# Small vector steps given a choice of engine, and the first batch's x kept as fp16 pairs, in a two-stage attention kernel

## The chip, the cores and the metric

The kernel runs on one core of one Trainium2 chip. The metric is the device time of one execution in microseconds (us); of several timed executions the median counts. Lower is better.

## The reference

Two stages follow each other. In the first, each of 8 batches and 8 heads has 512 tokens `x` and 32 state rows `state` of 64 elements; the tokens attend to the state rows and the state rows to the tokens. Their results, 544 rows for each batch, are the input of the second stage: a causal attention with four experts, each with its own q, k, v and output matrix, of which a gate picks two for each row.

```
scores  = x @ state.T / 8;   xread = softmax(scores) @ state
scores2 = state @ x.T / 8;   sread = softmax(scores2) @ x
x = concat([xread, sread])            # 8 x 544 x 512
logits = x @ w_gate                   # 4 experts, the best 2 are kept: weights w
for e in range(4):
    q, k, v = x @ wq[e], x @ wk[e], x @ wv[e]
    a  = softmax(causal(q @ k.T / 8))
    out += (e is picked) * w * (a @ v @ wo[e])
```

The q and k weights are large, so that the scores of the second stage spread widely and small errors in them would show. The kernel therefore carries nearly every operand of a matmul as a pair of fp16 numbers, a high part and the remainder, and multiplies pairs in three passes (high by high, high by low, low by high). "hi_lo" in the code makes such a pair: ScalarE rounds to the high part, VectorE (or GpSimd) subtracts it from the source to get the low part.

## The kernel before

**Names.** TensorE is PE in the profile, VectorE is DVE, ScalarE is ACT, GpSimd is POOL, and SP issues the DMAs. All instructions but a few constants are recorded first and issued by one loop in `Steps.run`, so nearly every instruction has line L265; tiles tell them apart.

**How the work is cut.** One batch is the unit. `front(b)` does the first stage for the 512 tokens of a batch (four blocks of 128, index `t`; two halves, index `u`) and forms the inputs of the second: `xn` is x as loaded (two buffers, one for each half of the tokens), `xh` its fp16 pair, `xT` the transposed pair, `bd` the transposed state pair; `eb` holds the scores and then the softmax of tokens over state rows, with `mb` the maxima and `sbm` the sums; `at` is that softmax transposed. Because the softmax has only 32 columns for each head, the products with wq, wk, wv and w_gate are first applied to the state (`gs`, "bank<-wn,bd" or, in the first batch, "bank<-p,bd" from the weights as loaded), and then `at` times `gs` gives v, k, q and the gate's logits `lg` ("bank<-gs,at", "bank<-at,gs"). `gate` turns logits into expert weights `wgt`, with `gs` also the name of its small sums. `m6` ("m<-wgt") masks q, `qf`/`qh`/`qm` are q, its pair and its transpose, `kt_` is k.

`side(b)` is the attention of state rows over tokens: `state_scores` gives `e2` ("e"), with `m2` ("m<-m") the scaled maxima and `s2` ("s") the sums, then `a2`, its transpose `a2t`, and the product with `xh`, kept in `xt_tail`.

`probs(b, unit)` does the second stage's scores for one block of tokens (or two): `mx` are the negated maxima of each row, `shifted` adds a constant to them, ACT takes exp with `mx` as bias and sums into `su`, `p` are the probabilities, `ph` their pair, and a DMA transpose gives `pt`. `su` is then inverted and multiplied with the expert weights to `c6` ("c<-su,wgt"). `reads` multiplies `pt` with v, weighs the result by `c6` (tile `z`), transposes it by DMA (`z<-zh`) and applies wo. `tail` does the same for the 64 state rows of two batches at a time; its tiles begin with t (`tmx`, `tqf`, `ptl`).

**First batch.** `whole = b < CFG["FB"]` is true for batch 0 alone. There x, the softmax and `gs` are kept whole in fp32 and multiplied in one fp32 pass, not in three fp16 passes; x is transposed on PE, straight from `xn` (lines 511 to 517), later batches' x by DMA. Since `side(0)` needs `xh` anyway, batch 0's pairs are made late, just before it (lines 675 to 677). The logits of batch 0 have a matmul step of their own (lines 624 to 628), ahead of the v products.

**What sets the order.** Three packed tables in `ORDER` (line 22) say in which order the recorded steps are issued, which way each step runs where `st.either` gave it several (for example ACT or DVE), and which buffer slot each tile gets. Each engine, and the SP queue with its DMAs, takes its own instructions strictly in that order; a step waits for the steps that wrote its inputs or last used its slot. Before the change the small steps, such as `shifted` (line 766) and the sums' epsilon (lines 571, 705, 756, 811), had one way only, VectorE.

Of the kernel before, what the change touches and what calls it, by code (L numbers as in the profile page):

```python
# [35 lines left out]
        "EL+t_zxoQ6vTfBgw%wpFmZV7L``Wi5_KV_CD@Y)n~_s<T8ay?1ua9N-W0+|uqAb%<;dKTwqQ6C?o2DN7e(V^_>+%f6kdrDFgkao09NWlF*yd"
        "u=57>~WAQFog`vC^S7SWhgH<^q=HWOTpS#m;*@khs8n3}U@{99wc-o7*buIR#d~DQ%NcJJiKR%BAC_wgVevTsh5kv&#H=jq90^FaX$_X@yK+"
        ")t67v#UZ0~4^zNxX=AGznk8?HFBZNI1EK)w!mGmqdIDBS;LXC5ibmj-{BAjBCp-jVOC1GRBgmT!WMIVX4WH@R+3FD_BQr@c|h}`=mCf;qjD^"
        "Q*tVvKyxTHr{zEnqjVfw_Dd$-#B*sPrRRAxi8AnHT0uu-GjHW7bX<<gR5~abxvos3Eqq9}@d2Dq^<+CQpqaE!GxH9fP77%_ucZ2N8nf_0+{3"
        "eI6)mEyyp-1SYTC(rIUCQWHMENt(^Wi!*?Auq;kC4ka`1j$PC<NtXHZTq#vAw`Z=_s&h&S>k%FU&?5Fh5kyqS)0Q7*$L<R};Ch;)ogb0mo`W"  # L40
        "jPWpp%NTfB2yB%h6$u3CzAb|RFX>^DaQ@u9A3v1au(N7TuCUwT%J!#VreXgHJNOoW7<ScNkiFB@njoakP6&Lw$ep8MeFIT9H2XLkZ$5RIW2d"
        "ksGN~YatKe;cDg4U=n$2VlX{$wXfZj#m*tG6lrwaakLyuQD<!44oYGT#MKVaRjI+~xUarbv%pzxa2L;Lv%qZ#PEZ5<)lu7PORynQbIGdd3)R"
        "I|t(gR5&7dVw1rgM~DPG~MUt9ALI)Z<;0UF!2yy2MB5B9FK8)PRrDWzHd2xFM&}YjTy_@FPj9*C|jR%XPU%H{_gN<3^lYdT@~3lpA!NZ&F)s"
        "%y}fIG~sr9gPU?0xy{Wuo!;c#)SmBfPj1c~IKB4bj(m*vP)p7$x2O|epsxHx4rn<!PIoz<wBpKgP<wM{zD<2NL|Sux>C4@?fOO}5bc+khA-y"
        "GqWFQxo7CeZHNGTc2rRBC{(DG76UdTPps9pG}T%?y$R$j|1c_t_64!w~}^juC*sASUne3vT7d40fDr61p?w{lG@N;G}Q_vnLM(08(zKFW2Cs"
        "r~sfMc2z(NiOPpxujQg2tU?GdR52sFs>#~G?reWnLLzZ=l~Am*!ol_aAv)svw1kr;%9nOtIH>OuGut;j^G)VUB5|Iy`^(_BL9+%Hj=-~56NU"
        "RZMNOkQ9Qx^$!`g>pE8M?%0&AklkBfd=BYNzGTU6fqc3!{&SOy2DSTJINHe*oFZHuDm#?yfNyq3bHEki|bgZ_N``SuI^JHr+OF4^8u{Of`i0"
# [12 lines left out]
        "=1p+3ROc~vj()jZ5Acy*uXHN2)*^vYhzYk6(2<NpCb5Wk)"  # L60
    ),
    (
        "c-pO%(H4Xt2t>X7|3`1Tof2KZz^n%&P-X_SH9a_<rz7Kg`cL27W=0RZke`KcTOru;8!P`mF}Dhn&%<?GNXBXOAU#Oq;!#r6z;Wh4CX&ERfqZ"
        ")L4O6^2LA~?3(zfBC;81|0vQ=px`qJz6HBkvIR15y5@?w-iRVW2ViOF^uTiv_ty@-0vqQW3n9n;>_)k=Y^s6<DO#eytZ5Tm&JS#6Vme^!vWe"
        ">~CFi{J#By*k||8=`&y%ZLER"
    ),
# [202 lines left out]
def state_read_then_moe_attention(ctx: ExitStack, tc: tile.TileContext, x, state, w_gate, wq, wk, wv, wo, out):  # L269
# [214 lines left out]
    def front(b):  # L484
# [190 lines left out]
        if whole:  # L675
            for t in range(T):
                parts_of_x(t)
# [339 lines left out]
```

## Time and profile before

| | |
|---|---|
| three timed executions | 331.65, 333.86 and 335.05 us; median 333.86 |
| the profiled execution | 330.36 us |
| its span in the trace | 328.6 us |
| outside the span | 330.36 - 328.6 = 1.8 us |
| instructions in the span | 9140 |
| busy: PE, DVE, ACT, POOL | 288.2, 270.1, 219.3, 159.5 us |

The span runs from the first to the last instruction that the profile shows. Busy time of an engine is the time in which at least one of its instructions was under way. A row of the timeline gives start and duration in us, engine, line, operation, tiles and count of merged instructions; in brackets stands how long the engine had been idle before it, and what released it. A row of grouped instructions ends with the total busy time, the mean duration in ns of one, and the idle time before them.

### The profile page before, as it was taken

What the parts mean: (1) busy time and instruction counts of PE and PEld (TensorE: products, weight loads), DVE (VectorE), ACT (ScalarE), POOL (GpSimd) and SP (SyncE); (2) the same over time, 40 slices, a digit from 0 to 9 for tenths busy, and PEclk for the clock granted to TensorE, in tenths of its full rate; (3) what the DMA queues carried; (4) which work ended last, traced back from release to release, by engine and by line L of the source; (5) the groups of instructions that cost most, each with busy time, mean ns of one, the idle gap of its engine ahead of it and who ended that gap; (6) DMA issues with size and microseconds to landing.
All of it is one profiled execution on the core that took longest, in us unless ns stands there. A gap on an engine that the chain in (4) does not pass through costs nothing.

```text
span 328.6 us, 9140 instructions
## 1 busy us (share of the span) xinstructions
PE 288.2 (88%) x3358; PEld 199.2 (61%) x3358; DVE 270.1 (82%) x819; ACT 219.3 (67%) x642; POOL 159.5 (49%) x199
## 2 busy tenths in 40 slices
PE   7959947998298998998897998997999899999882
PEld 6727726666256565865573677755775667576551
DVE  0388988989999999999999989898999968676420
ACT  2185555769467885877966869677868748647741
POOL 5043081369475578824884496365856510242100
PEclk9965985999699999999999999999999999999998
DMA  7905796998978799699999899989889958886973
GB/s 178 168 12 158 165 174 131 179 238 149 240 143 163 144 210 182 138 185 182 235 209 204 132 195 169 172 135 188 174 168 157 181 118 145 159 149 113 166 164 96
DMA packets 165540, 53.95 MB, mean 164 GB/s; under 512 B 144504, under 2 KB 160888, under 8 KB 165496
## 3 DMA queue, kind: packets, MB, share of 16 engines
q1 hardware_dynamic: 165496, 53.38, 87.5%
q8 instruction: 26, 0.43, 0.5%
q14 instruction: 18, 0.15, 0.1%
HBM read 11.02 MB, written 8.91 MB: 61 GB/s over the span
## 4 chain that ended last, share of the span: by engine, by line
DVE 24%; PE 19%; DMA 12%; ACT 10%; issue 6%; POOL 3%; POOLq 0%; SPq 0%; ACTq 0%; DVEq 0%
PE bank L265 19%; DMA a2t<-a 4%; DVE mx L265 3%; DMA pt<-ph 3%; DVE eb L265 3%; DMA xT<-xh 3%; ACT z L265 2%; DVE gs L265 2%; DVE sbm L265 2%; ACT xh L265 1%; DMA qm<-qh 1%; DMA z<-zh 1%; DVE et L265 1%; ACT p L265 1%; DVE z L265 1%
## 5 line engine op out<-in xcount | busy, mean ns | idle before, releaser
L265 PE MATMUL bank<-gs,at 128*128 128x260 f16 (+3 forms) x384 | 52.7, 288 | 1.6 <-DVE m L265 1.6
L265 PE MATMUL bank<-v,pt 128*128 128x192 f16 x480 | 44.9, 251 | 9.4 <-DMA pt<-ph 8.7
L265 PE MATMUL bank<-wo_n,z 128*128 128x512 f16 x192 | 46.0, 380 | 3.7 <-DMA z<-zh 3.7
L265 PE MATMUL bank<-kt,qm 128*128 128x128 f16 (+7 forms) x384 | 47.9, 301 | 1.1 <-DMA qm<-qh 0.9
L265 PEld LDWEIGHTS <-pt 128*128 128x128 f16 x480 | 40.3, 100 | 13.9 <-DMA pt<-ph 11.9
L265 ACT ACTIVATE p<-bank,mx 128x128 f32<-128x128 f32 (+3 forms) x64 | 33.4, 528 | 18.3 <-DVE mx L265 15.6
L265 PEld LDWEIGHTS <-at 128*128 128x128 f16 x336 | 31.7, 97 | 9.4 <-issue 3.8
L265 DVE TENSOR_REDUCE mx<-bank 128x1 f32<-128x128 f32 (+3 forms) x64 | 29.3, 478 | 5.5 <-PE bank L265 5.5
L265 POOL TENSOR_TENSOR z<-z 128x128 f32<-128x128 f32 x24 | 13.7, 572 | 39.8 <-ACT z L265 28.1
L265 POOL TENSOR_TENSOR ph<-p,ph 128x768 f16<-128x768 f32 (+1 forms) x13 | 24.1, 1855 | 16.2 <-ACT ph L265 10.2
L265 PEld LDWEIGHTS <-z 128*128 128x128 f16 x192 | 17.6, 98 | 23.3 <-DMA z<-zh 5.0
L265 PEld LDWEIGHTS <-qm 128*128 128x128 f16 (+1 forms) x384 | 23.2, 97 | 14.0 <-DMA qm<-qh 1.4
L265 ACT ACTIVATE z<-bank,c 128x64 f32<-128x64 f32 x126 | 29.4, 332 | 2.8 <-DVE z L265 2.2
L265 PE MATMUL bank<-at,gs 128*128 128x512 f16 (+1 forms) x92 | 25.3, 419 | 0.0
L265 ACT ACTIVATE o<-bank 128x512 f32<-128x512 f32 x34 | 20.5, 602 | 6.4 <-PE bank L265 6.3
L265 POOL TENSOR_TENSOR qh<-qf,qh 128x768 f16<-128x768 f32 x11 | 18.7, 1700 | 2.8 <-ACT qh L265 2.2
L265 ACT ACTIVATE ph<-p 128x768 f16<-128x768 f32 (+1 forms) x20 | 18.6, 931 | 1.3 <-DMA pt<-ph 0.9
L265 ACT ACTIVATE xh<-xn 128x512 f16<-128x512 f32 x32 | 19.3, 640 | 0.1
L265 ACT ACTIVATE gs<-bank 128x512 f16<-128x512 f32 (+3 forms) x36 | 14.4, 458 | 5.3 <-PE bank L265 5.2
L265 DVE TENSOR_TENSOR qf<-bank,m 128x384 f32<-128x384 f32 x32 | 16.5, 548 | 1.0 <-PE bank L265 0.6
L265 POOL TENSOR_TENSOR zh<-z,zh 128x256 f16<-128x256 f32 x19 | 14.0, 741 | 5.4 <-ACT zh L265 3.9
L265 POOL TENSOR_TENSOR eb<-eb,sbm 128x512 f32<-128x512 f32 x7 | 8.1, 1164 | 16.6 <-ACT bd L265 13.2
(189 smaller groups left out, 669.5 us busy)
## 6 DMA issues: line engine op xcount, KB each, us to landing
xn<-in_x_dram SPq DMA_DIRECT2D x16, 512.0 KB
out_dram<-o SPq DMA_DIRECT2D x64, 128.0 KB
sn<-in_state_dram SPq DMA_DIRECT2D x16, 32.0 KB
p<-in_moe_wo_dram SPq DMA_DIRECT2D x2, 256.0 KB
out_dram<-o SPq DMA_DIRECT2D x2, 256.0 KB
z<-zh SPq DMA_TRANSPOSE x29
xT<-xh SPq DMA_TRANSPOSE x28
p<-in_moe_wq_dram SPq DMA_DIRECT2D x1, 384.0 KB
```

Of the source, the lines that this page charges most:

```text
L265: f(**{k: v.ap() if isinstance(v, View) else v for k, v in kw.items()})
```

## The change

1. **Choice of engine.** Two helpers, `small` (a scale and an addition on a few numbers of each partition) and `pair` (a product of two small tiles), record steps that may run on DVE, ACT or POOL (`pair`: DVE or POOL). The steps on `mx`, `sbm`, `su`, `s2`, `m2`, `tmx`, the gate's sum, `c6` and the q mask `m6` use them or a like choice.
2. **First batch.** x is split into pairs at once for all batches; batch 0 transposes the pairs on PE (8 fp16 transposes for a block into one bank, two copies out of it), and its two score steps take the usual three fp16 passes. Softmax and `gs` of batch 0 stay in fp32.
3. **Logits with values.** In batch 0 the weights wv and w_gate go through one bank, as do wq and wk, and the logits come out of the v products as 4 further columns; the separate logits step is gone.
4. **Another order.** All three tables of `ORDER` are new.

```diff
+    def small(n, out, in_, add, mul=1.0):
+        st.either([("DVE", 0.065 + n * 0.00104, (nc.vector.tensor_scalar, dict(out=out, in0=in_, scalar1=add, scalar2=mul, op0=ALU.add, op1=ALU.mult))),
+                   ("ACT", 0.1 + n * 0.000833, (nc.scalar.activation, dict(out=out, in_=in_, func=AF.Copy, bias=add * mul, scale=mul))),
+                   ("POOL", 0.17 + n * 0.00084, (nc.gpsimd.tensor_scalar, dict(out=out, in0=in_, scalar1=add, scalar2=mul, op0=ALU.add, op1=ALU.mult)))])
+    def pair(n, **kw):
+        st.either([("DVE", 0.065 + n * 0.00104, (nc.vector.tensor_tensor, kw)), ("POOL", 0.24 + n * 0.001887, (nc.gpsimd.tensor_tensor, kw))])
...
         for t in range(T):
-            if whole:
+            parts_of_x(t)
+            if b < CFG["PX"]:
                 tp = bank("xt")
-                st.mm([(tp[HC[c], j * P:(j + 1) * P], xn[t // 2][:, 2 * j + c, t % 2 * D:(t % 2 + 1) * D], ident, True, True) for j in range(H // 2) for c in range(2)],
-                      (8, 4 * P, 128, 2), into=[xT[:, t]])
+                ts = tp.bitcast(F16).rearrange("p (a j q) -> p a j q", a=2, j=H // 2)
+                st.transposes([(ts[:, a, j, :], xh[t // 2][:, t % 2, a, j * P:(j + 1) * P]) for a in range(2) for j in range(H // 2)],
+                              identh, 0.43, into=[xT[:, t]])
                 marks["t"] = len(st.all) - 1
-                out_of_bank(512, xT[:, t].rearrange("p j q -> p (j q)"), tp, 128.0)
+                for a in range(2):
+                    kw = dict(out=xT[:, t, a], in_=ts[:, a])
+                    st.either([("ACT", 0.478, (nc.scalar.activation, dict(func=AF.Copy, scale=1.0, **kw))), ("DVE", 0.6, (nc.vector.tensor_copy, kw))])
...
-                if whole:
-                    st.mm([(scs[c][:, t * P + j * NS:t * P + (j + 1) * NS], xT[HC[c], t, j, :], bd32[HC[c], HJ[j]], True, True)
-                           for t in range(2 * u, 2 * u + 2) for j in range(H // 2) for c in range(2)], (16, 4 * NS, 64, 2), into=[eb])
-                    continue
...
-            dve(16, nc.vector.tensor_scalar, out=sm[:, r], in0=sm[:, r], scalar1=EPS, scalar2=2.0 ** -12, op0=ALU.add, op1=ALU.mult)
+            small(16, sm[:, r], sm[:, r], EPS, 2.0 ** -12)
...
-        if whole:
-            lp = bank("lg")
-            st.mm([m for t in range(T) for m in chain((lp[:, t * E:(t + 1) * E], at[:, g, tok[t]], gs[:, g, NW - E:NW]) for g in range(2))],
-                  (2 * T, 52, 128, 1))
-            act(T * E, lg.rearrange("p t e -> p (t e)"), lp[:, :T * E])
         for t in range(T):
             vp = bank("vp")
-            product(vp, tok[t], QK, QK + E * D if whole else NW, [v[:, :, t]])
-            if not whole:
-                act(E, lg[:, t], vp[:, E * D:E * D + E])
+            product(vp, tok[t], QK, NW, [v[:, :, t]])
+            act(E, lg[:, t], vp[:, E * D:E * D + E])
...
-            dve(12, nc.vector.tensor_scalar, out=m6[:, :, 1 - s], in0=wgt[:, :, 3 * s:3 * s + 3], scalar1=0.0, scalar2=0.5 ** 15, op0=ALU.is_gt, op1=ALU.mult)
+            st.either([("DVE", 0.078, (nc.vector.tensor_scalar, kw)), ("POOL", 0.18, (nc.gpsimd.tensor_scalar, kw))])
...
-            dve(1, nc.vector.tensor_scalar, out=m2[:, g:g + 1], in0=m2[:, g:g + 1], scalar1=2.0 ** -17, scalar2=None, op0=ALU.mult)
+            small(1, m2[:, g:g + 1], m2[:, g:g + 1], 0.0, 2.0 ** -17)
...
-        dve(2, nc.vector.tensor_scalar, out=s2, in0=s2, scalar1=EPS, scalar2=2.0 ** -14, op0=ALU.add, op1=ALU.mult)
+        small(2, s2, s2, EPS, 2.0 ** -14)
...
     def shifted(n, mx):
-        dve(n, nc.vector.tensor_scalar, out=mx, in0=mx, scalar1=LN, scalar2=None, op0=ALU.add)
+        small(n, mx, mx, LN)
...
-        dve(2 * nb, nc.vector.tensor_scalar, out=su, in0=su, scalar1=EPS * 2.0 ** 15, scalar2=None, op0=ALU.add)
+        small(2 * nb, su, su, EPS * 2.0 ** 15)
         dve(28, nc.vector.reciprocal, out=su, in_=su)
-        dve(6 * nb, nc.vector.tensor_tensor, out=c6, in0=su.unsqueeze(2).broadcast_to([P, 2 * nb, 3]),
+        pair(6 * nb, out=c6, in0=su.unsqueeze(2).broadcast_to([P, 2 * nb, 3]),
```

What the new tables do is seen in the instructions of each engine. Counted over the whole program, DVE has 821 instructions before and 722 now, ACT 556 and 582, POOL 204 and 255. Of the 144 small steps that were DVE's (`mx` 24, `m<-m` 16, `m<-wgt` 16, `sbm` 16, `su` 24, `s` 8, the gate's sum 12, `tmx` 4, `c<-su,wgt` 24), 36 stay there, 55 are on ACT and 53 on POOL. Of the larger steps, 10 more z products and 6 more `a` low parts are on DVE, and 30 z activations fewer on ACT.

The first place is the SP queue, in the first batch. `xn` rows are loads of x, `p` rows loads of weights, `sn` loads of state; `xn_88` and `xn_89` are the two buffers of x, so their second appearance loads batch 1. Before:

```order
L265 DMA sn_87<-in_state_dram 128x1x64
L265 DMA p_1_109<-in_moe_wk_dram 128x12x64
L265 DMA p_2_110<-in_moe_wv_dram 128x12x64
L265 DMA sn_87<-in_state_dram 128x1x64 x5
L265 DMA xn_88<-in_x_dram 128x8x128
L265 DMA xn_89<-in_x_dram 128x8x128
L265 DMA p_0_108<-in_moe_wo_dram 128x512
L265 DMA_TRANSPOSE xT_95<-xh_93 128x8x128
```

And now:

```order
L265 DMA p_1_111<-in_moe_wk_dram 128x12x64
L265 DMA p_0_110<-in_moe_wq_dram 128x4x64
L265 DMA xn_88<-in_x_dram 128x8x128
L265 DMA xn_89<-in_x_dram 128x8x128
L265 DMA sn_87<-in_state_dram 128x1x64 x4
L265 DMA xn_88<-in_x_dram 128x8x128
L265 DMA_TRANSPOSE xT_97<-xh_95 128x8x128 x2
L265 DMA p_0_110<-in_moe_wo_dram 128x512
```

The loads of batch 1 stand right behind the weights, and a third load of x stands ahead of the first transposes.

The second place is DVE at the start of the first batch, from its first step on data to the last subtraction of the maxima. `bd` is the state pair, `xh_93` and `xh_94` the pairs of the two halves of x. Before:

```order
L265 TENSOR_SCALAR xT_95<-bank_83 128x512
L265 TENSOR_SCALAR xT_95<-bank_84 128x512
L265 TENSOR_REDUCE mb_112<-bank_86 128x16
L265 TENSOR_REDUCE mb_112<-bank_85 128x16
L265 TENSOR_TENSOR eb_111<-bank_86,mb_112 128x512
L265 TENSOR_TENSOR eb_111<-bank_85,mb_112 128x512
```

And now:

```order
L265 SCALAR_TENSOR_TENSOR bd_90<-bank_79,bd_90 128x128
L265 SCALAR_TENSOR_TENSOR xh_93<-xn_88,xh_93 128x512 x2
L265 SCALAR_TENSOR_TENSOR xh_94<-xn_89,xh_94 128x512
L265 COPY xT_97<-bank_81 128x512
L265 SCALAR_TENSOR_TENSOR xh_94<-xn_89,xh_94 128x512
L265 COPY xT_97<-bank_83 128x512
L265 COPY xT_97<-bank_84 128x512
L265 TENSOR_REDUCE mb_114<-bank_86 128x16
L265 TENSOR_REDUCE mb_114<-bank_85 128x16
L265 TENSOR_TENSOR eb_113<-bank_85,mb_114 128x512
L265 TENSOR_TENSOR eb_113<-bank_86,mb_114 128x512
```

The four low parts of x, which stood among the later work, are now ahead of the first maxima, between the loads and the scores.

The third place is a step of `probs` in the middle of the kernel, the third block of tokens of batch 3 (its maxima are in `mx_154` before and in `mx_156` now). DVE before:

```order
L265 TENSOR_REDUCE mx_154<-bank_82 128x1
L265 TENSOR_REDUCE gt_0_123<-cmp_122 128x16
L265 TENSOR_REDUCE mx_154<-bank_85 128x1
L265 TENSOR_TENSOR ptl_197<-p_0_108,ptl_197 128x640
L265 SCALAR_TENSOR_TENSOR tsu_196<-tsu_196 128x1
L265 SCALAR_TENSOR_TENSOR a_0_146<-e_0_140,s_1_144,a_0_146 128x512
L265 TENSOR_SCALAR mx_154<-mx_154 128x2
```

The same step on ACT now:

```order
L265 ACTIVATE tmt_190<-bank_83 128x256
L265 ACTIVATE mx_156<-mx_156 128x2
L265 ACTIVATE p_2_112,su_160<-bank_86,mx_156 128x384
L265 ACTIVATE zh_175<-z_1_169 128x256
L265 ACTIVATE tq_192<-tqf_191 128x256
L265 ACTIVATE p_2_112,su_160<-bank_79,mx_156 128x384
```

The addition on `mx` has left DVE and stands on ACT directly ahead of the exponential that reads it.

More of the change, by code (lines that the diff above doesn't have):

```diff
@@ L59 @@
[L59 to L72 removed]
+        "c-jrrgJKX06adico0p9(+ja}fwr$(?(z0#awr$(Cd+&V2K_FldP%y{~1)vZ(02G995COtN9>@>*ASy(JNDvF+Lo|pCu^}o(hX9BIaUcdHfS3"
@@ L488, in front @@
         f32 = ("bitcast", (F32,), {})
[L490 removed]
+        bd = st.buf("bd", [P, 2, P], F16, bufs=2)
         tp = bank("tp")
[L492 removed]
+        st.transposes([(tp[:, :P], sn[:, b % 2].rearrange("p c d -> p (c d)"))], ident, 0.11, into=[bd])
+        hi_lo(P, bd[:, 0], bd[:, 1], tp[:, :P], 128.0)
         if whole:
[L494 removed]
+            bd32 = st.buf("bd32", [P, P], bufs=CFG["FB"])
             act(P, bd32, tp[:, :P], scale=128.0)
[L496 to L497 removed]
         xh = [st.buf("xh", [P, 2, 2, DM], F16, bufs=CFG["xh"], use=u) for u in range(2)]
[L500 to L501 removed]
+        xT = st.buf("xT", [P, T, 2, H // 2, P], F16, bufs=1)
         def parts_of_x(t):
@@ L618, in product @@
             if whole:
-                st.mm(chain((out[:, :n], at[:, g, t], gs[:, g, lo_:hi_]) for g in range(2)), (2, 4 * n, 128, 1), into=into)
+                st.mm(chain((out[:, :n], at[:, g, t], gs[:, g, lo_:hi_]) for g in range(2)), (2, 4 * n + 230, 128, 1), into=into)
             else:
@@ L646, in front @@
             if whole:
-                st.mm(chain((pp, gs[:, g, cols], at[:, g]) for g in range(2)), (2, 4 * S, 128, 1), into=[kt_[:, :, pr, :]])
+                st.mm(chain((pp, gs[:, g, cols], at[:, g]) for g in range(2)), (2, 4 * S + 230, 128, 1), into=[kt_[:, :, pr, :]])
             else:
@@ L653, in front @@
         for s in range(2):
-            dve(12, nc.vector.tensor_scalar, out=m6[:, :, 1 - s], in0=wgt[:, :, 3 * s:3 * s + 3], scalar1=0.0, scalar2=0.5 ** 15, op0=ALU.is_gt, op1=ALU.mult)
+            kw = dict(out=m6[:, :, 1 - s], in0=wgt[:, :, 3 * s:3 * s + 3], scalar1=0.0, scalar2=0.5 ** 15, op0=ALU.is_gt, op1=ALU.mult)
+            st.either([("DVE", 0.078, (nc.vector.tensor_scalar, kw)), ("POOL", 0.18, (nc.gpsimd.tensor_scalar, kw))])
         for u in range(2):
@@ L674, in front @@
                 load_wo(marks["l"])
-        if whole:
-            for t in range(T):
-                parts_of_x(t)
-        side(b, bd32 if whole else bd, xT, xh, whole)
+        side(b, bd, xT, xh)
         st.behind = None
@@ L755, in gate @@
         dve(m, v.tensor_reduce, out=s1, in_=t2, axis=AX.X, op=ALU.add)
-        dve(n, v.tensor_scalar, out=s1, in0=s1, scalar1=EPS, scalar2=0.5, op0=ALU.add, op1=ALU.mult)
+        small(n, s1, s1, EPS, 0.5)
         dve(n, v.reciprocal, out=s1, in_=s1)
```

119 lines of the change are left out of this document (57 added, 62 removed).

## The prediction

> **What bounds the kernel now.** I read the page first: busy shares, the slices of the span, the chain of work that ended last. Then a table of five stretches of the span, the timelines of the stretches where PE stood idle, and the groups of DVE instructions by shape.
>
> ```profile
> PE 288.2 (88%) x3358; PEld 199.2 (61%) x3358; DVE 270.1 (82%) x819; ACT 219.3 (67%) x642; POOL 159.5 (49%) x199
> ...
> DVE  0388988989999999999999989898999968676420
> ...
> PEclk9965985999699999999999999999999999999998
> ...
> DVE 24%; PE 19%; DMA 12%; ACT 10%; issue 6%; POOL 3%; POOLq 0%; SPq 0%; ACTq 0%; DVEq 0%
> ```
>
> Two engines are near full, and DVE holds more of the chain than PE. The slices say when: DVE is idle in the first two (to 16 us), at nine tenths until some 240 us, and falls off at the end. The granted clock of PE is low only early. The stretches make that exact (columns: stretch, its length, busy us and instructions of PE, PE weight loads, DVE, ACT, POOL, then clock, DMA share, GB/s):
>
> ```profile
> 0.00:24.00 24.00, 17.98 (x254) 13.62 (x254) 9.72 (x21) 10.36 (x23) 8.17 (x35) 0.90 0.60 122
> 24.00:60.00 36.00, 29.05 (x334) 22.34 (x327) 31.54 (x82) 20.15 (x48) 11.40 (x14) 0.73 0.74 155
> 60.00:240.00 180.00, 161.84 (x1984) 110.34 (x1983) 170.41 (x538) 134.78 (x409) 115.46 (x120) 0.98 1.00 181
> 240.00:310.00 70.00, 68.39 (x720) 46.93 (x718) 55.52 (x174) 48.36 (x149) 24.05 (x30) 1.00 0.83 150
> 310.00:329.00 19.00, 10.92 (x84) 6.00 (x79) 2.91 (x8) 5.62 (x15) 0.45 (x1) 0.93 0.60 125
> ```
>
> So there are three regimes. To 60 us the first batch is a chain of waits. From 60 to 240 DVE is busy for 170.4 of 180 us and PE idle for 180 - 161.8 = 18.2: DVE sets the pace and PE pays. From 240 to 310 PE is busy for 68.4 of 70; nothing that DVE saves there shortens it. A gain must come from the first two.
>
> **The change part by part: the first batch.** These rows of the timeline carry it:
>
> ```profile
> 8.47 1.97 PE L265 MATMUL bank<-ident,xn 128*64 128x128 f32 x32
> ...
> 15.03 1.29 DVE L265 TENSOR_REDUCE mb<-bank 128x16 f32<-128x512 f32 x2 [3.84 <-PE bank L265]
> ...
> 22.13 1.96 PE L265 MATMUL bank<-xT,bd 64*32 64x512 f32 x16
> 24.02 3.58 PE L265 MATMUL bank<-gs,at 128*128 128x4 f32 x16
> ...
> 27.70 0.64 PE L265 MATMUL bank<-gs,at 128*128 128x256 f32 x1
> ...
> 44.99 0.46 PE L265 MATMUL bank<-bd,xT 64*128 64x32 f16 x24 [1.97 <-DMA xT<-xh]
> ...
> 51.46 2.02 PE L265 MATMUL bank<-ident,eb 128*128 128x128 f32 x8 [4.97 <-DVE eb L265]
> ...
> 58.24 2.83 PE L265 MATMUL bank<-gs,at 128*128 128x260 f16 x24
> ...
> 88.06 3.06 PE L265 MATMUL bank<-v,pt 128*128 128x192 f16 x18 [7.15 <-DMA pt<-ph]
> ```
>
> From the second half of x on PE (8.47) to the first maxima (15.03) are 6.6 us. Now the pairs come first. They are no new work, only earlier, in a stretch where DVE and ACT were idle; their prices:
>
> ```profile
> L265 ACT ACTIVATE xh<-xn 128x512 f16<-128x512 f32 x32 | 19.3, 640 | 0.1
> ```
>
> ```profile
> L265 DVE SCALAR_TENSOR_TENSOR xh<-xn,xh 128x512 f16<-128x512 f32 x23 | 15.9, 723 | 0.0
> ```
>
> The last two blocks need two high parts on ACT (2 x 0.64), one low part after the last of them (0.72) and, ahead of it on DVE, one copy out of a bank, at most another 0.7: 2.7 us. Transposing one block is put at 1.0, the fp32 row's 1.97 halved for two blocks; two copies at 0.6 each (the size of the `xh` activation) at 1.2; the second half's 48 scores in fp16 at 0.9, twice the 24 at 44.99. That is 5.8 for 6.6, so -0.8; bounds are -2 (half of each estimate) and +1.5 (copies and low parts one after the other).
>
> The logits step is simpler. From 24.02 to 27.70 PE did nothing but 128x4 products in fp32, 3.7 us on the path to the first v products. In their place the v products get 4 columns more of 256, 1.6% of them. I take -3.6; bounds -3.7 and 0, the latter if `gs` or `at` comes late instead. The state scores at 22.13 shrink too, but PE waits around them, so nothing is counted.
>
> Third, the loads of batch 1.
>
> ```profile
> SPq L265 <- DVE xh L265: 11.5, 3, 5.5
> ```
>
> ```profile
> 23.50 3.93 SPq L265 DMA_DIRECT2D xn<-in_x_dram  x2
> ```
>
> Both x buffers stayed taken until DVE had made batch 0's low parts, so SP issued batch 1's x only at 23.50, and everything behind it waited in SP's queue too. With the pairs made at some 11 us the buffers are free 12 us earlier, and these loads stand right behind the weights. What this can save is what PE lost to batch 1 later: 1.97 us at 44.99 for its `xT` and 4.97 at 51.46 for its softmax, 6.9 in all. That softmax also needs DVE, which was 88% busy there (31.54 of 36). I take -3, with bounds -6.9 and 0. The first batch gives -0.8 - 3.6 - 3.0 = -7.4.
>
> **The small steps.** 108 of the 144 leave DVE. The groups by shape:
>
> ```profile
> L265 DVE TENSOR_SCALAR mx<-mx 128x2 f32<-128x2 f32 x16 | 5.9, 371 | 0.0
> ...
> L265 DVE TENSOR_SCALAR gs<-gs 128x4 f32<-128x4 f32 x8 | 3.0, 378 | 0.1
> ...
> L265 DVE TENSOR_SCALAR su<-su 128x2 f32<-128x2 f32 x16 | 2.7, 171 | 1.5 <-ACT p L265 1.2
> ...
> L265 DVE TENSOR_SCALAR m<-wgt 128x12 f32<-128x12 f32 x16 | 2.7, 185 | 0.1
> ...
> L265 DVE TENSOR_SCALAR sbm<-sbm 128x16 f32<-128x16 f32 x16 | 2.6, 179 | 0.0
> ...
> L265 DVE TENSOR_TENSOR c<-su,wgt 128x6 f32<-128x6 f32 x16 | 2.6, 162 | 0.1
> ...
> L265 DVE TENSOR_SCALAR s<-s 128x2 f32<-128x2 f32 x8 | 2.1, 267 | 0.6 <-ACT e L265 0.6
> ...
> L265 DVE TENSOR_SCALAR mx<-mx 128x4 f32<-128x4 f32 x8 | 1.2, 155 | 0.0
> ```
>
> 14 `mx` of two numbers at 0.371 are 5.2 us, 8 `gs` 3.0, 10 `su` 1.7, 14 `m<-wgt` 2.6, 10 `sbm` 1.8, 8 `c` 1.3, 7 `s` 1.9, the other 37 at the 0.155 of the last row 5.7: 23.2 us of durations. Durations overlap, though, and some are long for another reason:
>
> ```profile
> 62.88 0.15 DVE L265 TENSOR_SCALAR mx<-mx 128x4 f32<-128x4 f32 x1
> 62.95 0.16 DVE L265 TENSOR_TENSOR gt<-lg,gs 128x16 f32<-128x16 f32 x1
> ...
> 178.42 1.59 DVE L265 TENSOR_SCALAR mx<-mx 128x2 f32<-128x2 f32 x1
> ```
>
> ```profile
> 178.33 1.66 POOL L265 TENSOR_TENSOR ph<-p,ph 128x768 f16<-128x768 f32 x1 [1.39 <-ACT ph L265]
> ```
>
> The next instruction starts 0.07 after one that lasts 0.15, so each takes some 0.08 less than its duration: 23.2 - 108 x 0.08 = 14.6 us of DVE. And the two-number step that took 1.59 ended at 180.01, as POOL's row ended at 179.99: DVE stood behind a POOL instruction, on the step that every exponential of that block waits for. The Trainium skill (SBUF — State Buffer, "Who interferes with whom") says that such a `tensor_scalar` takes the port pair shared with GpSimd as an exclusive lock, and that ACT never waits for it; the trace agrees with 1.59 against 0.155 us.
>
> The larger steps that changed engine nearly cancel on DVE, by these rows and the `xh` row:
>
> ```profile
> L265 DVE SCALAR_TENSOR_TENSOR a<-e,s,a 128x512 f16<-128x512 f32 x9 | 9.1, 1012 | 0.9 <-POOL a L265 0.6 <-ACT a L265 0.2
> ...
> L265 DVE TENSOR_TENSOR z<-bank,c 128x192 f32<-128x192 f32 x22 | 7.5, 343 | 5.5 <-PE bank L265 4.7 <-ACT z L265 0.8
> ```
>
> 10 z (+3.4) and 6 `a` (+6.1) come, and softmax products, `ph` and `zh` low parts go, each at 0.5 to 1.2: about +2 on balance. DVE loses some 13 us net, of which 170.4/270.1, or 8, lie in its full stretch. PE's 18.2 idle us there would let all 8 through; since PE also waits for DMAs (7.15 at 88.06), I take -6, with bounds -9 and 0.
>
> **What it costs elsewhere.** The nearest rows for the moved steps are a four-number activation on ACT and a sixteen-number product on POOL:
>
> ```profile
> L265 ACT ACTIVATE lg<-bank 128x4 f32<-128x4 f32 x28 | 4.8, 196 | 2.3 <-DVE v L265 1.2 <-PE bank L265 1.1
> L265 ACT ACTIVATE z<-bank,c 128x64 f32<-128x64 f32 x126 | 29.4, 332 | 2.8 <-DVE z L265 2.2 <-PE bank L265 0.5
> ```
>
> ```profile
> L265 POOL TENSOR_TENSOR wgt<-gt,gs 128x16 f32<-128x16 f32 x6 | 1.7, 284 | 15.3 <-DVE gs L265 13.9 <-DVE c L265 1.4
> ```
>
> ACT gets 55 x 0.196 = 10.8 us and loses 30 z of 0.332, 10.0: even, at 67% busy. POOL gets 53 x 0.284 = 15, from 49% to some 53%. What is new is the crossing: a step that DVE did between two of its own now waits in another queue, and what is queued behind it on ACT (the next exponentials and roundings) or POOL waits with it. `mx` and `tmx` on ACT add none, since ACT's exponential is the reader; `sbm` and `s` return to DVE's reciprocal and add one each. I take +1, with bounds 0 and +5.
>
> **The sum.** -7.4 - 6 + 1 = -12.4: the span goes from 328.6 to 316.2, the execution to 318.0. The profiled execution of before (330.36) lies 3.5 below the median of the timed ones (333.86); the same distance would give 321.5. I take 320, between the two.
>
> **The rivals.**
>
> *PE becomes the bound throughout.* Then the waits at 44.99 and 51.46 go wholly (-6.9), PE's 18.2 idle us shrink to the 4 that DMAs cause, and with -4.4 from the first batch's start and logits the median loses 25.5: 308 us. For it: PE is already gapless after 240. Against: DVE would have to keep up at some 95% busy with PE at 98%. Chance 0.13.
>
> *DVE gets nothing back.* POOL's 53 added instructions hold up DVE's two-input steps from SBUF as much as the moved ones were held up; `a` already means 1.01 us against 0.72 for the `xh` step of the same size. Then only the first batch counts: 333.9 - 7.4 + 1 = 327. Against: half of the moved steps went to ACT. Chance 0.15. The skill's Perfetto Trace Analysis ("Optimizing Scalar/DVE Operations") warns of just this: since GpSimd and DVE share a read port, offloading between them might not help.
>
> *The gain is hidden.* The first batch's lead is lost again in SP's strict queue: transposes issued earlier meet batch 1's loads, and DVE's savings only lengthen its own idle time while PE waits for DMAs as at 88.06. Some 332. Chance 0.10.
>
> *Slower: the crossings.* In each batch about eight moved steps (three `mx`, two `sbm`, `s`, the gate's sum, a mask) stand in a chain that PE waits for, 64 in all. If each waits 0.2 us behind a longer instruction, the 12.4 is gone (64 x 0.2 = 12.8); at 0.35 it is 22.4, some 10 us slower, 343. A single step behind a POOL row such as the 1.66 would cost that much. Against: on ACT `mx` stands directly ahead of its reader, and the steps that were held up by POOL on DVE no longer are. Chance 0.10.
>
> *The change does not move the work.* The instructions of each engine show that it does; no chance of its own.
>
> **How the numbers follow.** The forecast has 0.52. About 1%, or 3.3 us, is what a measurement tells from no change. Faster by more than that are the forecast, the PE-bound case and the front-only case, 0.52 + 0.13 + 0.15 = 0.80; same 0.10; slower 0.10. The range goes from 307 (the PE-bound case) to 333 (the hidden one), and leaves the slow case out.
>
> **What would show each step.** Right: first maxima on DVE before 15 us, v products of the first batch near 23.5 and not 27.7, no 128x4 fp32 products; batch 1's x issued before 15; the first 128x260 products of batch 1, at 58.24 before, near 50; DVE's busy sum near 255 with no `mx` step over 1 us; PE idle for about 12 us, not 18, in the full stretch. Wrong: first maxima after 16 us; ACT or POOL as the releaser of long DVE waits on `sbm` or `s`; DVE still at 95% for 180 us, or its `a` and `ph` steps longer than before.

## The result, and the profile after

The changed kernel takes 320.31 us (median of four executions, 319.38 to 322.01), the kernel before 332.75 us beside it (four executions, 329.63 to 335.05). The ratio is 0.966, with a 95% interval from 0.957 to 0.975. Ratios, here and below, leave out executions more than 1.5% above the fastest of their kernel. The forecast was 320 us, between 307 and 333. The profiled execution of the changed kernel is 320.58 us, its span 318.8.

Now the page of the changed kernel: busy sums, DVE and the granted clock in 40 slices, the chain of work that ended last by engine.

```profile
PE 281.8 (88%) x3350; PEld 191.4 (60%) x3350; DVE 258.9 (81%) x720; ACT 219.7 (69%) x668; POOL 173.6 (54%) x250
...
DVE  1789998998999979989999999875988978787420
...
PEclk9959998999799999999999999997999999999998
...
PE 33%; DMA 16%; DVE 12%; ACT 4%; issue 3%; POOL 3%; SPq 1%; POOLq 0%; DVEq 0%; ACTq 0%
```

DVE lost 11.2 us of busy time (forecast: some 13, to 255), ACT kept its own, and POOL gained 14.1 (forecast 15). On the chain of work DVE fell from 24% to 12%, and DMAs stand ahead of it. Of the 9.8 us by which the span is shorter, 6.4 are busy time of PE (288.2 to 281.8) and 3.4 its idle time; the granted clock over the whole span is 0.97, before 0.95. The same five stretches as before, with the same columns:

```profile
0.00:24.00 24.00, 16.52 (x269) 12.17 (x270) 14.27 (x29) 13.98 (x29) 8.85 (x37) 0.86 0.82 187
24.00:60.00 36.00, 29.71 (x353) 18.45 (x351) 34.32 (x89) 23.46 (x72) 17.83 (x28) 0.95 0.83 155
60.00:240.00 180.00, 165.34 (x2010) 113.16 (x2011) 159.49 (x458) 138.87 (x429) 122.83 (x152) 0.98 0.99 177
240.00:310.00 70.00, 67.93 (x714) 46.79 (x712) 50.36 (x146) 41.58 (x139) 24.09 (x35) 1.00 0.87 159
310.00:329.00 19.00, 2.32 (x11) 0.87 (x9) 0.42 (x1) 1.83 (x4) 0.00 (x0) 0.88 0.16 41
```

In the full stretch DVE fell from 170.4 to 159.5 us, PE's idle time only from 18.2 to 14.7. In the first 60 us DVE and ACT do far more than before (DVE 48.6 in place of 41.3 us), and the granted clock of the second stretch rose from 0.73 to 0.95. The timeline of PE, and two rows of DVE and SP:

```profile
22.13 2.35 PE L265 MATMUL bank<-gs,at 128*128 128x260 f32 x8
...
30.88 0.77 PE L265 MATMUL bank<-bd,xT 64*128 64x32 f16 x48 [1.55 <-DMA xT<-xh]
...
45.08 1.27 PE L265 MATMUL bank<-ident,eb 128*128 128x128 f32 x8 [1.78 <-POOL eb L265]
46.97 2.10 PE L265 MATMUL bank<-kt,qm 128*128 128x128 f16 x12 [0.62 <-ACT xh L265]
...
50.35 0.84 PE L265 MATMUL bank<-gs,at 128*128 128x260 f16 x6
...
79.94 1.88 PE L265 MATMUL bank<-wo_n,z 128*128 128x512 f16 x6 [3.24 <-DMA z<-zh]
```

```profile
13.19 1.29 DVE L265 TENSOR_REDUCE mb<-bank 128x16 f32<-128x512 f32 x2 [1.20 <-PE bank L265]
```

```profile
13.69 2.15 SPq L265 DMA_DIRECT2D xn<-in_x_dram  x2
```

The first maxima come at 13.19 (before 15.03), the first v products at 22.13 with the logits in them (before 27.70), batch 1's x is issued at 13.69 (before 23.50), and the first 128x260 products of batch 1 start at 50.35, where the prediction had "near 50" (before 58.24). The waits of 4.97 and 7.15 us are gone; 3.24 is the longest after the start. By 50 us the kernel is 7.9 us ahead, and at the end 9.8 (span against span); in between the two orders differ too much to compare single steps. So most of the lead is there early, though the prediction put 5 of its 12.4 us into the small steps, most of which come later. One sign missed: PE's idle time in the full stretch was to be 12 us.

The groups by shape say what the moved steps cost (x of them | busy us, mean ns | idle before):

```profile
L265 ACT ACTIVATE mx<-mx 128x2 f32<-128x2 f32 x12 | 2.4, 201 | 3.6 <-DVE mx L265 3.4
```

```profile
L265 POOL TENSOR_SCALAR m<-wgt 128x12 f32<-128x12 f32 x14 | 4.0, 296 | 6.3 <-DVE wgt L265 5.6 <-DVE gt L265 0.7
```

```profile
L265 DVE SCALAR_TENSOR_TENSOR a<-e,s,a 128x512 f16<-128x512 f32 x15 | 11.7, 780 | 0.1
...
L265 DVE TENSOR_TENSOR c<-su,wgt 128x6 f32<-128x6 f32 x8 | 4.6, 573 | 0.0
...
L265 DVE RECIPROCAL sbm<-sbm 128x16 f32<-128x16 f32 x16 | 3.8, 240 | 0.6 <-POOL sbm L265 0.5
...
L265 DVE RECIPROCAL gs<-gs 128x4 f32<-128x4 f32 x8 | 1.4, 171 | 1.3 <-ACT gs L265 1.1 <-POOL gs L265 0.2
```

0.20 us on ACT and 0.30 on POOL, as the prediction took from its nearest rows (0.196 and 0.284). DVE's waits for steps that now cross are small: 0.5 us in all for `sbm`, 1.3 for the gate's sum. Of the steps that stayed on DVE, `c` grew: it means 0.573 us where it meant 0.162. Its mean is raised most by two steps of 1.25 and 1.75 us, and the longer one ended at 148.89 as a product on POOL (`ph`) ended at 148.86; `su` and `sbm` on DVE kept their lengths (0.172 and 0.189).

### The profile page after: what moved, and what is told of

It reads as the page before. It is cut to its first block, busy times and chain, and to the rows that moved or that the text cites. A ratio compares the mean times of both kernels' runs of the same rounds, so it can differ in the third digit from the quotient of the medians.

```text
span 318.8 us, 9081 instructions
## 1 busy us (share of the span) xinstructions
PE 281.8 (88%) x3350; PEld 191.4 (60%) x3350; DVE 258.9 (81%) x720; ACT 219.7 (69%) x668; POOL 173.6 (54%) x250
## 4 chain that ended last, share of the span: by engine, by line
PE 33%; DMA 16%; DVE 12%; ACT 4%; issue 3%; POOL 3%; SPq 1%; POOLq 0%; DVEq 0%; ACTq 0%
PE bank L265 33%; DMA a2t<-a 5%; DMA qm<-qh 3%; DMA tpt<-ptl 3%; DMA pt<-ph 2%; DMA out_dram<-o 1%; DMA z<-zh 1%; DVE mx L265 1%; DVE gs L265 1%; ACT z L265 1%; SPq L265 1%; DVE z L265 1%; DVE xh L265 1%; DVE qf L265 1%; ACT p L265 1%
## 5 line engine op out<-in xcount | busy, mean ns | idle before, releaser
L265 PE MATMUL bank<-kt,qm 128*128 128x128 f16 (+7 forms) x384 | 50.9, 315 | 4.4 <-DMA qm<-qh 2.5
L265 PE MATMUL bank<-gs,at 128*128 128x260 f16 (+3 forms) x368 | 49.5, 284 | 0.0
L265 POOL TENSOR_TENSOR ph<-p,ph 128x768 f16<-128x768 f32 (+1 forms) x17 | 31.5, 1858 | 8.5 <-ACT ph L265 6.1
L265 ACT ACTIVATE z<-bank,c 128x64 f32<-128x64 f32 x96 | 22.9, 327 | 7.3 <-PE bank L265 2.9
L265 POOL TENSOR_TENSOR eb<-eb,sbm 128x512 f32<-128x512 f32 x14 | 16.0, 1150 | 20.8 <-DVE bd L265 12.7
L265 POOL TENSOR_TENSOR qh<-qf,qh 128x768 f16<-128x768 f32 x12 | 20.5, 1707 | 4.3 <-ACT qh L265 4.0
L265 ACT ACTIVATE xh<-xn 128x512 f16<-128x512 f32 x32 | 19.3, 626 | 4.5 <-DMA xn<-in_x_dram 3.6
L265 POOL TENSOR_TENSOR zh<-z,zh 128x256 f16<-128x256 f32 x24 | 17.1, 716 | 7.7 <-ACT zh L265 6.3
L265 POOL TENSOR_TENSOR z<-z 128x128 f32<-128x128 f32 x19 | 10.6, 560 | 17.3 <-DVE z L265 10.6
L265 DVE SCALAR_TENSOR_TENSOR xh<-xn,xh 128x512 f16<-128x512 f32 x26 | 17.7, 693 | 2.8 <-ACT xh L265 2.7
L265 ACT ACTIVATE ph<-p 128x768 f16<-128x768 f32 (+1 forms) x20 | 18.1, 904 | 0.3
L265 DVE TENSOR_TENSOR z<-bank,c 128x192 f32<-128x192 f32 x32 | 10.9, 349 | 8.9 <-PE bank L265 6.6
```

The costliest lines, as they stand in the source:

```text
L265: f(**{k: v.ap() if isinstance(v, View) else v for k, v in kw.items()})
```

## The experiments

All times below are medians of a run's executions, interleaved with executions of the kernel before on the same chip; "ratio" is to those, with its interval. In the code, "..." marks what is left out. Against the changed kernel's 0.966 a ratio is read with both intervals.

**Run e1: small steps back on DVE, in the new order.**

```diff
         assert len(ways) == len(self.all)
+        ways = bytes(0 if n in self.small else w for n, w in enumerate(ways))
```

(`self.small` lists the 144 steps that `small`, `pair` and the mask's choice record; way 0 is DVE.)

> The changed kernel with all 144 small steps back on DVE, in the order of steps of the changed kernel; all else as changed. If the move of the small steps was worth what the prediction took (-6 for DVE's relief, +1 for the crossings), this run loses 5 us: some 325 us beside 320. If the gain comes from the first batch alone, as the two traces suggest (the changed kernel is 8 to 9 us ahead by 60 us and 10 us ahead at the end), it stays at 320, within 2. If the crossings cost more than DVE's relief brings, it is faster: 317 or less. DVE's busy sum should rise from 258.9 to some 275 us in all three cases.

Measured: 330.88 us, ratio 1.002 [0.998, 1.006]; DVE's busy sum is 282.2 us (in an execution of 334.12 us). The whole gain is gone, the first batch's too, though its code is unchanged. That is more than any of the three theories had: the move is worth about 12 us in this order (0.036 of 331; both intervals together give 8 to 15). The clock alone is not the gain: the executions in e1's ratio had a mean granted clock of 0.97, as the changed kernel had, those of the kernel before beside them 0.94, and their times are the same.

**Run e2: the same engines in the kernel before.**

```diff
+        ways = bytearray(ways)
+        for n, e in zip(self.small, ENGINES, strict=True):
+            ways[n] = int(e)
```

> The kernel before, its own order of steps, with the same 108 small steps on ACT and GpSimd as in the changed kernel; nothing else changed. If DVE sets the pace from 60 to 240 us and the move relieves it, the time falls by about 5 us, to 328 beside 333. If the move buys nothing, it stays within 2 of 333. If the crossings cost and only the new order of steps pays for them, it is slower than before: 336 or more, with ACT or POOL as the releaser of new DVE waits on sbm, s or c.

Measured: 329.40 us, ratio 0.996 [0.991, 1.000]. The same 108 steps on the same engines are worth 1.5 us here (0 to 3), not 5. In the profiled execution the first transposes of x, ahead of any moved step, take 3.68 us where they took 1.97, and PE starts the second half of x 1.4 us later (9.82 against 8.47); at the end it is 1.3 ahead (span 327.3). Without that start the move would have brought some 2.7 there; whether the other executions start late too is not on record.

**Run e3: the small steps left out.**

```diff
             s = self.all[n]
+            if n in self.small and self.all[n]["ways"][0][2][0][1]["out"].buf.tag in ("mx", "tmx", "su", "sbm", "s2", "gs1"):
+                continue
```

> The kernel before with 88 of its small steps left out (the shifts of the maxima, the sums' EPS and scale for softmax, state read, gate and expert probabilities), so it computes other numbers. It shows what DVE's relief is worth at most, with no crossing at all. If DVE sets the pace as the prediction had it, DVE loses some 12 us of its own time and the time falls by 6 to 9 us, to 324 to 327. If PE's idle time in the full stretch is set by something else (transposes through DMA, the chain of each batch), it falls by 0 to 3 us.

Measured: 328.47 us, ratio 0.994 [0.991, 0.998], 1.8 us (1 to 3). 88 of the 144 steps are left out, and DVE's busy sum is 257.8 us, about that of the changed kernel. This is the run that decides on "DVE sets the pace". Its row for the full stretch (PE, weight loads, DVE, ACT, POOL, clock, DMA share, GB/s):

```profile
60.00:240.00 180.00, 164.59 (x1973) 111.70 (x1972) 160.80 (x475) 134.39 (x405) 112.81 (x118) 0.95 1.00 180
```

DVE has 160.8 us there in place of 170.4, nearly as little as in the changed kernel, and nothing crosses to another engine; the time hardly moves. PE's idle time there falls by 2.8 us (18.2 to 15.4), but in this execution its busy time grows by as much (161.8 to 164.6), at a granted clock of 0.95 in place of 0.98; with the clock left aside the relief would be worth some 3 us, still not 6. What PE waits for in that stretch, first in the kernel before, then in this run (us in total, times, the longest):

```profile
PE bank L265 <- DMA pt<-ph: 8.7, 2, 7.2
PE bank L265 <- DMA z<-zh: 2.1, 2, 1.8
PE bank L265 <- DMA a2t<-a: 1.7, 1, 1.7
PE bank L265 <- DVE m L265: 1.6, 1, 1.6
PE bank L265 <- DVE qf L265: 1.3, 2, 1.1
PE bank L265 <- DMA xT<-xh: 1.2, 1, 1.2
```

```profile
PE bank L268 <- DMA pt<-ph: 7.9, 1, 7.9
PE bank L268 <- DMA z<-zh: 2.1, 1, 2.1
PE bank L268 <- DMA a2t<-a: 2.1, 1, 2.1
PE bank L268 <- DMA xT<-xh: 1.2, 1, 1.2
PE bank L268 <- DVE qf L268: 0.8, 1, 0.8
```

With the small rows that are not shown, 13.9 of the 18.2 us ended with a DMA transpose, and here 14.2 do. Of the waits that ended with DVE (1.6, 1.3 and a further 0.6) 0.8 is left: that is what e3 takes away. The longest wait stays because of the queue; run e3's own rows:

```profile
77.45 1.32 DVE L268 TENSOR_TENSOR ph<-p,ph 128x768 f16<-128x768 f32 x1
...
87.33 3.06 PE L268 MATMUL bank<-v,pt 128*128 128x192 f16 x18 [7.95 <-DMA pt<-ph]
```

```profile
74.76 5.76 SPq L268 DMA_TRANSPOSE xT<-xh  x3
80.58 0.56 SPq L268 DMA_DIRECT2D xn<-in_x_dram  x1
81.25 2.86 SPq L268 DMA_TRANSPOSE pt<-ph  x1
```

The low part of `ph` is done at 78.8; its transpose stands behind three `xT` transposes and an x load, is issued at 81.25 and has landed when PE resumes at 87.33. The DMA engines' share in the stretch is 1.00, in the row that the prediction quoted for DVE.

**Run e4: the logits apart again**, in the changed kernel.

```diff
-            product(vp, tok[t], QK, NW, [v[:, :, t]])
...
+                st.mm([m for u in range(T) for m in chain((vp[:, E * D + u * E:E * D + (u + 1) * E], at[:, g, tok[u]], gs[:, g, NW - E:NW]) for g in range(2))
+                       if t == 0] + chain((vp[:, :E * D], at[:, g, tok[t]], gs[:, g, QK:QK + E * D]) for g in range(2)), ...)
```

> The changed kernel with the first batch's logits as products of their own again (fp32, 128x4, ahead of the first value product, in the same bank). The prediction put this term at 3.6 us, the duration of the row in the trace of before; that row ran at a granted clock of 0.50, so at full clock it would be 1.8. Prediction as on record: 323.6. Size by the clock: 322. If the time of PE in the first batch is hidden behind DVE or DMAs: 320, within 1.

Measured: 319.98 us over the three executions in the ratio (321.57 over all six), ratio 0.968 [0.962, 0.974], against 0.966 [0.957, 0.975]: no difference that can be told. The intervals alone leave room for some -3 to 4 us, so the rows have to decide. PE's, from an execution of 326.37 us:

```profile
22.03 3.78 PE L265 MATMUL bank<-gs,at 128*128 128x4 f32 x24
...
27.48 1.98 PE L265 MATMUL bank<-at,gs 128*128 128x512 f32 x4
```

The step after the first two blocks of values starts at 27.48, 0.8 us later than in the changed kernel (26.65), and at the first 128x260 products of batch 1 0.5 us are left (50.86 against 50.35). What makes this execution longer comes after that.

**Run e5: the new order with all the old engines.** A string gives each step that exists in both kernels the way that it had before:

```diff
+        for n, w in zip([n for n, s in enumerate(self.all) if len(s["ways"]) > 1], BEFORE, strict=True):
+            ways[n] = ways[n] if w == "." else int(w)
```

> The changed kernel in its own order of steps, but each step that exists in both kernels on the engine it had before: the small steps on DVE, and also the products, rounded parts and z steps as before. What is left of the change is the first batch (pairs first, logits with the values) and the order. Run e1 left DVE 282 us busy, since the changed order also gives DVE ten z products and six a parts more; here DVE should have some 270 to 273, as before. If e1 lost its 10 us to DVE's load, this run gets part of it back: the prediction's own account (first batch -7.4) gives 325, a ratio to before of 0.978. If the new order does not work without the moved small steps at all, it stays at the time of before or above: ratio 1.00 or more.

Measured: 350.54 us, ratio 1.063 [1.059, 1.066], and on the page:

```profile
PE 291.1 (84%) x3350; PEld 194.7 (56%) x3350; DVE 293.8 (84%) x824; ACT 219.9 (63%) x642; POOL 155.0 (44%) x199
```

My account of e1 (ten z products too many for DVE) falls: with the old engines DVE is busier still, 293.8 us where much the same steps in the old order took 270.1. Much the same instructions, but some are longer: `c` of six numbers means 0.418 us where it meant 0.162 before, `sbm` 0.373 (0.179), `su` of two 0.318 (0.171); `mx` of two, 0.371 before, is not, at 0.319. The trace says why. Maxima and sums over rows aside, 15 DVE steps with at most 16 results for each partition last 0.9 us or more, and each of them ends within 0.06 us of the end of an instruction on POOL (an `sbm` of 1.59 at 47.29, POOL's `qh` at 47.26). e1 has 14 of these, the kernel before 7, e2 2 and the changed kernel 5. An order made for one choice of engines puts DVE's steps beside POOL's in another choice. How much of the 20 us these holds make up was not tried by itself.

**Run e6: the clock kept up in the kernel before.**

```diff
+        [(self.nc.tensor.matmul, dict(out=group[0][0], lhsT=z, rhs=z, start=True, stop=True, skip_group_check=True)) for z in warm] + ...
-                               for t in range(T)], ident, 0.44, into=[at[:, u]])
+                               for t in range(T)], ident, 0.44, into=[at[:, u]], warm=[zeros] * 28 if whole and u == 0 else ())
```

> The kernel before with 28 more idle-time products of zeros on PE, put ahead of the first batch's transposes of its softmax (where PE stood idle from 16.8 to 20.3 us and the granted clock fell to 0.50 until 33.0 us). If the clock follows PE's activity, it stays at 1.00 there, the 12.7 us of products from 20.3 to 33 shrink by up to 6.4 us, and the first batch's PE work ends near 36 in place of 40.75. If that reaches the end, the time falls by 4 to 6 us (ratio 0.98 to 0.985): then most of the first batch's gain was the clock. If something else sets the pace later (the DMA queue, as run e3 suggests), it falls by less than 2 us.

Measured: 330.63 us, ratio 1.001 [0.998, 1.004]. In the profiled execution the products did their work; the stretch, and PE's rows after it:

```profile
20.00:33.00 13.00, 12.50 (x72) 8.78 (x73) 12.42 (x31) 11.34 (x29) 5.86 (x7) 1.00 0.38 107
```

```profile
22.76 1.95 PE L265 MATMUL bank<-gs,at 128*128 128x4 f32 x16
...
31.60 3.62 PE L265 MATMUL bank<-gs,at 128*128 128x256 f32 x16
35.15 0.19 PE L265 MATMUL bank<-bd,xT 64*128 64x32 f16 x1
...
40.10 0.50 PE L265 MATMUL bank<-bd,xT 64*128 64x32 f16 x24 [3.65 <-DMA xT<-xh]
...
50.40 2.02 PE L265 MATMUL bank<-ident,eb 128*128 128x128 f32 x8 [5.15 <-DVE eb L265]
```

The clock is 1.00, the logits step takes 1.95 us where it took 3.58, and batch 1's scores can begin at 35.15, 5.6 us earlier than before (40.75). Then PE waits 3.65 for batch 1's `xT` and 5.15 for its softmax, and the transposes of that softmax start at 50.40, 1.1 us earlier. At the end nothing is left. In this kernel PE's time in the first batch was not on the path; the waits say that batch 1's x and its softmax were.

**Run e7: the clock kept up in the changed kernel.**

```diff
-                st.mm([(gp[HJ[j], ...
+                st.mm([(gps[0][:, :P], zeros, zeros, True, True)] * (8 if f == 2.0 else 16) +
+                      [(gp[HJ[j], ...
```

> The changed kernel with 8 and 16 products of zeros on PE ahead of the two groups that make the first batch's value and query/key factors, where PE waits 0.9 and 1.2 us for the weights' DMAs and the clock then falls to 0.50 from 16 to 22.6 us. If the clock stays at 1.00, PE has up to 2.9 us less to do there: 317 to 319 beside 320. If DVE and the DMAs set the pace of the first batch, 320 within 1. If the added products stand in the way of the real ones, 321.

Measured: 323.74 us, ratio 0.979 [0.975, 0.984]: slower than the changed kernel by some 4 us, the intervals just touching. The added products stood in nobody's way: the groups behind them start at 14.10 and 16.68, in the changed kernel at 14.29 and 16.78. PE is 1.4 us ahead at its second group of values (23.07 against 24.43), and then waits:

```profile
32.56 0.82 PE L265 MATMUL bank<-bd,xT 64*128 64x32 f16 x48 [3.23 <-DMA xT<-xh]
```

Here PE reaches this product 1.7 us later than in the changed kernel (30.88), because the last two `xT` transposes, issued at almost the same time (25.26 and 25.90), took 3.69 in place of 3.05 us in SP's queue. Why they did is open. But this is not where the run loses: at the first 128x260 products of batch 1 PE is ahead again (49.62 against 50.35). It falls behind from 64.5 us on, first at a wait of 1.03 us for ACT's `p`, and the span ends 3.7 us longer (322.5 against 318.8); what the added products have to do with that is open.

**Run e8: batch 1's x late.** One small write into its buffer, and three moves in the order:

```diff
+        for move, behind in (([len(self.all) - 1, 272, 273], 155), ([277, 280, 286, 283], 151), ([278, 281, 532, 287, 282, 279], 89)):
+            order = [n for n in order if n not in move]
+            at = order.index(behind) + 1
+            order[at:at] = move
...
+    fill(late[0][:, 0, :1], 0.0)
```

> The changed kernel with batch 1's x loaded some 8 us later: a small write of GpSimd into its buffer, queued behind GpSimd's work at 21 to 22 us, holds the two loads back (they were issued at 13.7), and batch 1's rounded pairs stand behind other steps of ACT and DVE accordingly. The prediction put the early loads at 3.0 us (0 to 6.9). By that, the time rises by 3 (ratio to before 0.975). If x is not what batch 1 waits for, it stays at 320; if all that batch 1 gained at its scores (12 us) came from these loads, it rises by 5 to 8.

Measured: 326.85 us, ratio 0.989 [0.984, 0.993], 0.0225 above the changed kernel: 7.4 us, with both intervals between 4 and 11.

```profile
21.04 6.59 SPq L270 DMA_DIRECT2D xn<-in_x_dram  x3
```

```profile
37.07 0.82 PE L270 MATMUL bank<-bd,xT 64*128 64x32 f16 x48 [3.09 <-DMA xT<-xh]
```

The loads are issued 7.3 us later, batch 1's second score step comes 6.2 us later (37.07 against 30.88), batch 1's first 128x260 products 5.0 later (55.34 against 50.35), and the end 7.4 by the ratio or 5.7 by the profiled spans (324.5 against 318.8). Of the parts of the first batch that were tried by themselves, this one is on the path. The price is an upper one, since the rest of the order was left as it was: PE also waits 3.3 us for ACT's `e`, which now stands behind the late pairs in ACT's queue.

**Runs e9 to e12: orders made anew.** Since e2 and e5 show that an order belongs to its engines, four kernels got orders from one procedure, each for its own engines: both first batches, with and without the moved small steps. Of the three tables only the first changes; e10 and e11 take the choice of engines from e2 and e1:

```diff
 ORDER = (
     (
-        "c-jrrgJ...
+        (the order found for this kernel)
```

> One of four kernels whose order of steps was sorted anew, each for its own engines and by one and the same procedure (random moves of single steps within their engine's queue, kept when a rough account of durations, of the port that VectorE and GpSimd share and of one DMA queue gets shorter). This one: the kernel before, its first batch and its engines unchanged, only its order new. It is the base for the other three. If the kernel before was held up by its order, it is faster than before: ratio 0.97 to 0.985. If the procedure is worth nothing on the chip: 1.00 or more, and then the four only tell something among themselves.

> Second of the four: the kernel before with the 108 small steps on ACT and GpSimd (as in run e2), its order sorted anew for that. If the moved steps are worth what the prediction took (-5 us) once the order fits them, it is 5 us faster than e9. If their worth in the changed kernel lay in the order alone, it is within 2 us of e9.

> Third of the four: the changed kernel with all small steps on DVE (as in run e1), its order sorted anew for that. Run e1 lost 10 us against the changed kernel. If that was the load on DVE, most of it stays: ratio to before 0.99 or more, 5 us or more above e12. If it was an order made for other engines, it goes: within 2 to 3 us of e12, ratio 0.97 to 0.975, and the rest of the gain is the first batch's.

> Last of the four: the changed kernel with its own engines, only the order sorted anew by the same procedure. If the procedure is as good as the order that the change came with, the ratio to before is 0.966 or less; a ratio above 0.975 says how much the change's own order is better than what this procedure finds. Against e9, all of the change but the skill of its order: by the prediction's terms some 12 us.

| | small steps on DVE | 108 of them moved | difference |
|---|---|---|---|
| first batch as before | e9: 347.69, 1.053 [1.047, 1.058] | e10: 342.17, 1.036 [1.031, 1.041] | -5.5 |
| first batch as changed | e11: 346.30, 1.049 [1.044, 1.054] | e12: 335.75, 1.019 [1.013, 1.024] | -10.6 |
| difference | -1.4 | -6.4 | all: -11.9 |

The procedure makes worse orders than either kernel came with, by some 17 us (0.053 and 0.052 in the ratios), so its times say something among themselves only. There the moved steps come out at 5.5 to 10.6 us and the new first batch at 1.4 to 6.4, and each at more when the other is there. The 1.4 can't be told from nothing, and the clock is in these numbers too: to 60 us the profiled executions of e9, e10, e11 and e12 had 0.75, 0.83, 0.77 and 1.00. Each cell is one order that the procedure found; how far another attempt would lie from it was not measured.

## Why the prediction was right, and where its account was not

**The total.** -12.4 us were summed for the span, and 9.8 came (328.6 to 318.8); by medians 12.4 (332.75 to 320.31), by the ratio 11. The forecast of 320 and its range held. Its account of where the time would come from held only in part, and that the total came so close is luck: a term that came to nothing (logits) and two that came out more than twice as large (batch 1's loads, and the small steps in this order) don't add up to it, because each depends on what else is changed.

**Pairs first (-0.8).** The first maxima came 1.8 us earlier, inside the bounds of -2 and +1.5. What that is worth at the end was not tried by itself; e6 says that an earlier PE alone is worth nothing there in the kernel before.

**Logits (-3.6).** This step failed. "3.7 us on the path to the first v products" was true of those products, but they are not on the path to the end: e6 made PE 5.6 us faster in just this place and gained nothing, and e4 put the step back at a cost that can't be told from nothing, 0.5 us by 50 us. The row was also read at the wrong price: at a clock of 1.00 it lasts 1.95.

**Batch 1's loads (-3.0).** The mechanism was right and its size too small: e8 puts it at 7.4 us (4 to 11) as an upper price. The two waits of PE (1.97 and 4.97) bound what PE loses at those two places, but the lateness of x also moves what is queued behind it on ACT and SP.

**The small steps (-6).** The durations, the 13 us that DVE would lose (11.2 came) and the prices on ACT and POOL were right. "DVE sets the pace and PE pays" failed: e3 takes 9.6 us off DVE in that stretch of the kernel before, and the time falls by 1.8. PE's idle time there ended with DMA transposes for 13.9 of 18.2 us, which the profile of before could tell; the prediction read the share of busy time and not what PE's waits ended with. What the moved steps are worth is not one number: 1.5 us in the old order, some 12 in the new one, 5.5 and 10.6 in the orders made anew. In the kernel before they buy little, as PE waits for DMAs there; in the new order, which fills DVE's queue otherwise, they can't be taken back.

**The crossings (+1).** Right in size as far as DVE's waits show it: 0.5 us for `sbm` and 1.3 for the gate's sum, over the whole span.

**The rivals.** "DVE gets nothing back" did not come, though half of its mechanism is there: `c` on DVE went from 0.162 to 0.573 us, while `a` fell from 1.012 to 0.780, and DVE steps held up by POOL became fewer (7 to 5). The Trainium skill's page on SBUF (SBUF — State Buffer, "Who interferes with whom") describes the exclusive lock of that port; the traces agree: all 15 small steps of 0.9 us or more in e5 end with an instruction on POOL, and so do the 7 of the kernel before. "The gain is hidden" (332) describes the kernel before with the small steps moved, at 329.4: as far as e3's waits show, the DMA queue hides the gain unless the order changes too.

**Open.** How the new order's worth splits among the port, DVE's own time and the DMA queue; why two `xT` transposes took longer in e7, and what e7 loses after 64 us; what the early pairs are worth by themselves.

## What to carry to other kernels

Before crediting an engine's relief, look at what the waits of the engine that ends last end with, and leave the work out altogether in one run: that bounds the gain in the order as it stands (here 1.8 us, where 6 had been expected). In a kernel whose order is written out for its engines, the choice of engines and the order are one change: the moved steps alone brought 1.5 us, the new order with the old engines cost 20, and all together brought 11 to 12. A product's duration is read together with the granted clock of its stretch, and a shorter chain in one batch counts only if the next batch's inputs are there to follow it.

## What the runs showed of the hardware

The granted clock of PE did not go by gaps alone. In the kernel before it fell to 0.50 at 19.3 us, some 2.6 us after PE's last product (which ended at 16.8), and stayed there until 32.9 us, though PE was busy almost without a break from 20.3 and wholly from 22.7 on; in the changed kernel it fell at 16.0 without any gap over 1.24 us and came back at 22.8. In run e6 it fell at 14.7 after 3.4 us in which PE was never idle, and came back at 18.1. Stretches of before, then of after (PE busy first, clock third from the end):

```profile
16.00:20.00 4.00, 0.76 (x17) 0.16 (x4) 3.87 (x10) 3.05 (x9) 0.56 (x1) 0.91 0.09 21
20.00:33.00 13.00, 12.74 (x50) 8.22 (x51) 10.47 (x25) 8.41 (x21) 5.44 (x7) 0.50 0.37 101
```

```profile
13.00:16.00 3.00, 1.34 (x45) 0.58 (x37) 2.78 (x5) 0.77 (x2) 0.00 (x0) 1.00 0.91 188
16.00:17.00 1.00, 0.22 (x8) 0.22 (x16) 1.00 (x3) 0.98 (x4) 0.00 (x0) 0.50 0.78 210
17.00:22.60 5.60, 5.60 (x65) 2.66 (x51) 4.74 (x10) 4.17 (x9) 3.09 (x6) 0.50 0.73 179
```

In the first half of those 13 us (to 27.7) stood fp32 transposes, products with 64 rows and products of 4 columns, after that fp32 products of 256 and 512 columns; with 28 products of zeros ahead of them the same instructions ran at 1.00 (run e6, one execution). The three stretches at 0.50 last 13.6, 6.8 and 3.4 us, all multiples of 3.4. The Trainium skill (TensorE: Matmul & The Clock Gate, "What's actually happening") gives a free-running window of that length, one busy window until the clock is whole and one idle window until it is halved. The length of the window fits these stretches. What counts as busy does not go by PE's busy time: the clock stayed at 0.50 for 10.2 us with PE busy throughout (before, 22.7 to 32.9), and it fell after a window without a gap (e6).
